# First batch: roots pair by pair, the later value maxima loaded behind the fifth pair and spread through DRAM at once

## The chip, the cores and the metric

The kernel runs on one core of one Trainium2 chip. The metric is the device time of one execution, in microseconds (us): the kernel before takes 1167.9 us, the median of 3 runs (1166.9 to 1169.97). Times of the trace count from the start of the profiled execution's span. The engines are PE (matrix products), ACT (activations and copies), DVE (vector operations), POOL (here short vector operations and the issue of some transfers) and SP (issue of most transfers). Each engine takes its instructions strictly in the order of its own list, so an instruction that waits holds up everything behind it on that engine.

## The reference

Three layers follow each other. The inputs q, k, v are (4, 12, 448, 64): 4 batches, 12 heads, 448 positions.

```python
def rmsnorm(x, g):
    rms = np.sqrt(np.mean(x * x, axis=-1, keepdims=True) + 1e-06)
    return x / rms * g
q_n, k_n = (rmsnorm(q, g_q), rmsnorm(k, g_k))
scores = scale * np.matmul(q_n, k_n.transpose(0, 1, 3, 2))
scores = scores - np.max(scores, axis=-1, keepdims=True)
attn = np.exp(scores)
attn = attn / (np.sum(attn, axis=-1, keepdims=True) + 1e-09)
x = np.matmul(attn, v)            # to (1792, 768)
h = x @ w_in                      # moe: 768 -> 2048 -> 768
x = (h * (1.0 / (1.0 + np.exp(-1.702 * h)))) @ w_out
h = x @ w_in2                     # moe2: 768 -> 2048 -> 768
out = (np.maximum(h, 0.0) + alpha * np.minimum(h, 0.0)) @ w_out2
```

The weights of the layers come as 64-bit words and are turned into single precision on the chip.

## The kernel before

**Stages.** Attention works on pairs of heads, six pairs in a batch, 24 in all. Batch 0 runs in single precision, the other three with numbers split into two half-precision parts. The first 205 us or so hold all of batch 0's attention, and beside it the conversion of the first layer's two weights (`weights`, named w1i and w1o in the trace; each piece of a row is loaded by SP at line 222, turned on ACT at line 147 and on DVE at lines 163 and 164, and reduced at line 244). From there on PE multiplies through the layers, with the attention of batch b + 1 laid between the products of batch b.

**Roots of a pair.** `normalize` takes the sums of squares of a pair's q and k (ACT line 401, DVE line 403) and then takes the reciprocal roots on POOL: one addition (line 404), one starting value (line 407) and three rounds of four short instructions (lines 411 to 414), 14 instructions in all. For batch 0 the roots go to `prep_pair`, which multiplies q and k by them on DVE (line 438, the tile qn), transposes the products on PE (lines 445 and 447) and copies them out on ACT (line 448). Before the change the first and the second pair have roots of their own, and the third and fourth, and the fifth and sixth, share a set of 14 instructions with twice the columns.

**The maxima of v.** Batches 1 to 3 need one scale each: the largest absolute value of v, rounded down to a power of two (mv), and a number made of its reciprocal (av). `v_scale` loads a batch's v in 8 pieces of 168 KB from POOL's queue (line 310, tile vst, two buffers), and ACT reduces each piece to a column (line 311). So a piece's load waits for the piece two before it to be reduced. `v_scales` then reduces the 8 columns on DVE, and `partition_max` spreads the maximum over the 128 partitions by a diagonal matrix on DVE (line 117, tile diag), a product with ones on PE (line 119, tile pm) and a reduction on DVE (line 120). The first use of av for batch 1 is `split` of a pair's v (tile vs), at 190.6 us.

**Order.** The code is written as generators that are stepped in turn, and a scheduler puts the instructions of each engine in an order, from the code's order, priorities and modelled times. The loads of v's pieces are written late in the code, with `issue_after(rooted[1].ins)`: they may be issued once the second pair's roots are done. The scheduler puts them as early as that lets it. On SP, the loads of w1o's 32 half rows stand one behind the other; each waits for one of four buffers.

Of the kernel before, what the change touches and what calls it, by code (L numbers as in the profile page):

```python
# [9 lines left out]
F32 = mybir.dt.float32  # L10
# [4 lines left out]
ALU = mybir.AluOpType  # L15
AX = mybir.AxisListType.X

EXP_MASK = 0x7F800000
VN = 8
# [16 lines left out]
SQB = 2  # L36
# [20 lines left out]
def attention_moe_kernel(  # L57
# [17 lines left out]
    nc = tc.nc  # L75
    B, H, S, D = q.shape
# [4 lines left out]
    NP = H // 2  # L81
# [5 lines left out]
    const = ctx.enter_context(tc.tile_pool(name="const", bufs=1))  # L87
    big = ctx.enter_context(tc.tile_pool(name="big", bufs=1))
    dram = ctx.enter_context(tc.tile_pool(name="dram", bufs=1, space=bass.MemoryType.DRAM))
    small = ctx.enter_context(tc.tile_pool(name="small", bufs=2))  # L90
# [11 lines left out]
    def pow2floor(dst, src):  # L102

        nc.vector.tensor_scalar(out=dst, in0=src, scalar1=1e-30, scalar2=None, op0=ALU.max)  # L104
        nc.vector.tensor_scalar(
            out=dst.bitcast(I32), in0=dst.bitcast(I32), scalar1=EXP_MASK, scalar2=None, op0=ALU.bitwise_and
        )

    def scaled_reciprocal(dst, src, c):

        nc.vector.tensor_scalar(out=dst, in0=src, scalar1=1.0 / c, scalar2=None, op0=ALU.mult)
        nc.vector.reciprocal(out=dst, in_=dst)

    def partition_max(dst, col):

        diag = small.tile([128, 128], BF16, tag="diag", name="diag", bufs=1)
        nc.vector.tensor_scalar(out=diag, in0=ident, scalar1=col, scalar2=None, op0=ALU.mult)
        pm = ps_m.tile([128, 128], F32, tag="m", name="pm")
        nc.tensor.matmul(out=pm, lhsT=ones, rhs=diag, start=True, stop=True)
        nc.vector.tensor_reduce(out=dst, in_=pm, op=ALU.max, axis=AX)  # L120
# [133 lines left out]
    def later_rows(w, d, other):  # L254

        nj = w.shape[1]
        return lambda j: w[:, j + d].rearrange("p e n -> p (e n)").bitcast(F32) if j + d < nj else other(j)
# [9 lines left out]
    att_p = att.enter_context(tc.tile_pool(name="att_p", bufs=2))  # L267
# [5 lines left out]
    g_col = const.tile([128, 1], F32, name="g_col")  # L273
    mv = const.tile([128, B], F32, name="mv")
    av = const.tile([128, B], F32, name="av")

    def gains():
        gq = small.tile([128, D], F32, tag="gq", name="gq", bufs=1)
# [18 lines left out]
    def v_scales(b, col):  # L297
        one = small.tile([128, 1], F32, tag="vone", name="vone")
        nc.vector.tensor_reduce(out=one, in_=col, op=ALU.max, axis=AX)
        pow2floor(one, one)  # L300
        partition_max(mv[:, b:b + 1], one)
        scaled_reciprocal(av[:, b:b + 1], mv[:, b:b + 1], 2.0 ** 13)

    def v_scale(b):
        flat = v[b].rearrange("h s d -> (h s d)").rearrange("(p n) -> p n", p=128)
        n = flat.shape[1] // VN
        col = small.tile([128, VN], F32, tag="vcol", name="vcol")
        for i in range(VN):
            t = raw_p.tile([128, n], F32, tag="vst", name="vst")
            nc.gpsimd.dma_start(out=t, in_=flat[:, i * n:(i + 1) * n])  # L310
            nc.scalar.activation(out=t, in_=t, func=AF.Abs, accum_out=col[:, i:i + 1])
        v_scales(b, col)

    raws = {}
    rawv = {}
# [67 lines left out]
    rooted = {}  # L383
# [295 lines left out]
    def first_pairs():  # L679

        steps = attention([4 * P + r for P in range(NP) for r in range(2)])
        for i, _ in enumerate(steps):
            P, r = divmod(i, 2)
            if P >= NP:
                yield
                continue
            if r == 0:
                prep = prep_pair(P + 1) if P + 1 < NP else iter(())
            next(prep, None)
            if r == 0 and P % 2 == 0 and P + 2 < NP:  # L690
                normalize(P + 2, P + 3)
            if r == 1:
                if P + 1 + QKB < NP:
                    load_qk(P + 1 + QKB)
                if P + 3 < NP:
                    load_v(P + 3)
            yield
# [456 lines left out]
    if True:  # L1154
        make_identity(nc, ident)
        nc.vector.memset(ones, 1.0)
        nc.vector.tensor_copy(out=identf, in_=ident)
        load_qk(0)
        gains()
        load_v(0)  # L1160
        load_qk(1)
        load_v(1)
        g0 = big.tile([128, KF, 2, S], F16, tag="g", name="g0")
        stage = g0.rearrange("p m e t -> p (m e t)").bitcast(F32)
        parts = stage[:, 0:R1I * 1024].bitcast(I32).rearrange("p (i n t) -> p i n t", i=R1I, t=2)
        raw1o = g0.rearrange("p m e t -> p m (e t)").bitcast(I32)[:, KF - 4 * R1O:, FIRST:].rearrange("p m (n t) -> p m n t", t=2)

        def num1i(j):
            if j == KD - 1:
                return stage[:, 5120:5120 + FF]  # L1170
            return held.bitcast(F32)[:, (j - 3) * FF:(j - 2) * FF]

        def num1o(j):
            if j == KF - 2:
                return att_p.tile([128, 2 * NT2 * D], F32, tag="ph", name="num1o", bufs=PHB)[:, 0:DM]
            return raw_p.tile([128, 2 * NT2 * D], F32, tag="qk", name="num1o", bufs=QKB)[:, 0:DM]

        w1i_steps = weights(
            moe_w_in, "w1i", lambda: w1i, later_rows(w1i, 3, num1i), lambda t: parts[:, t % R1I], 4, R1I, 2.0 ** -14, scales,
            G1I  # L1180
        )
        w1o_steps = weights(
            moe_w_out, "w1o", lambda: w1o, later_rows(w1o, 2, num1o), lambda t: raw1o[:, 4 * (t % R1O):4 * (t % R1O) + 4], 2,
            R1O, 2.0 ** -25, scales, G1O
        )
        next(w1i_steps)
        normalize(0)
        for _ in prep_pair(0):
            pass
        for P in range(2, 1 + QKB):  # L1190
            load_qk(P)
        load_v(2)
        normalize(1)
        for _ in first_pairs():
            for _ in range(W_RATE):
                next(w1i_steps, None)
        for _ in w1i_steps:
            pass
        v_scales(0, v0)
        first_x()  # L1200
        moe1_scales(0)
        for P in range(NP, NP + 2):
            load_qk(P)
            load_v(P)
        n1o = 0
        steps = attention([4 * P + r for P in range(NP) for r in range(2, 4)])
        for i, _ in enumerate(steps):
            pairs = max(0, (i - LAG + 1) // 2)
            rows = KF - 2 if pairs >= 4 else (HOLD + pairs * HELD) // (2 * DM) - 2
            while n1o < min(1 + 2 * rows + 3 * (rows // 2), (i + 1) * W1O_RATE, 57):  # L1210
                next(w1o_steps)
                n1o += 1
            if i >= M_AT and i - M_AT < KF:
                first_in(slice(0, FIRST), i - M_AT, g0, None)
            if i == VS_AT:
                for b in range(1, B):
                    with tc.issue_after(rooted[1].ins):
                        v_scale(b)
        while n1o < 57:
            next(w1o_steps)  # L1220
            n1o += 1
        for m in range(len(range(2 * NP + LAG)) - M_AT, KF):
            first_in(slice(0, FIRST), m, g0, None)
        with tc.issue_after(loads["w1o"][W1O_HOLD].ins):
            normalize(NP, NP + 1)
            for _ in prep_pair(NP):
                pass
            load_qk(NP + 2)
            load_qk(NP + 3)
            load_v(NP + 2)  # L1230
        att_steps = other_batches()
        done = 4 * NP
        late = late_weights(ctx, att)
        for b in range(B):
            last = min(NU, 4 * NP * (b + 2)) + LAG
            first = done
            got = None
            for i, _ in enumerate(moe1(b) if b else first_moe1(g0)):
                lead = 0 if b else B1_AT
                want = first + (last - first) * min(1.0, max(0.0, i + 1 - lead) / (PACE[b] * TICKS - lead))  # L1240
                while done < min(want, NU + LAG):
                    next(att_steps)
                    done += 1
                if b == B - 1:
                    for _ in range(1 if i < 2 * KF else 2):
                        if got is None or i >= 2 * KF:
                            got = next(late, None)
        second_layer(late)
# [30 lines left out]
```

## Time and profile before

| what | value |
|---|---|
| median of 3 runs | 1167.9 us (1166.9 to 1169.97) |
| the profiled execution's own time | 1169.73 us |
| its span, first to last instruction | 1168.0 us |
| mean granted clock of PE | 0.961 |
| PE busy, 292 to 1168 us | 857.2 of 876 us |
| PE busy, 0 to 205 us | 145.6 of 205 us |

The first 205 us are unlike the rest. From 292 us on PE is busy 98% of the time, so there the order of the other engines matters little. In the first 205 us PE stands for 59 us, and DVE (168.3 us) and ACT (142.4 us) are busy beside it. The profile attributes a wait to the instruction that came last.

### The profile page before, as it was taken

How to read it: one execution, taken by the hardware profiler on the slowest of the kernel's cores; microseconds unless marked ns; L12 is line 12 of the kernel's file. 1: busy time of each engine (PE TensorE's matmuls, PEld its weight loads, DVE VectorE, ACT ScalarE, POOL GpSimd, SP SyncE). 2: the span in 40 equal slices, each digit the busy share in tenths (PEclk: the TensorE clock that was granted, in tenths of full speed). 3: DMA queues.
4: the chain of work that ended last, by engine and by line, in shares of the span. 5: the costliest groups of instructions: out<-in, count | busy, mean ns of one | idle time of the engine just before them, and what ended most of it. 6: DMA issues, size and time to landing. Idle time of an engine off the chain costs nothing.

```text
span 1168.0 us, 18355 instructions
## 1 busy us (share of the span) xinstructions
PE 1072.6 (92%) x6755; PEld 586.6 (50%) x6755; DVE 810.1 (69%) x1407; ACT 682.0 (58%) x1396; POOL 169.6 (15%) x336
## 2 busy tenths in 40 slices
PE   3587779778998999999999999999999999999998
PEld 1243447743444445545555455444444477666665
DVE  6979987897788976567633957499977222978351
ACT  4789666576888886578733554256545323645220
POOL 3321001575543432210000000000000000000000
PEclk9677889998999999999999999999999999999999
DMA  7975542358898876665555801555533413353011
GB/s 244 273 213 143 148 136 71 89 100 165 173 175 171 148 121 143 139 120 97 102 123 155 302 4 52 201 202 195 183 103 120 138 68 120 100 179 105 29 32 31
DMA packets 235274, 158.05 MB, mean 135 GB/s; under 512 B 167728, under 2 KB 214448, under 8 KB 235184
## 3 DMA queue, kind: packets, MB, share of 16 engines
q1 hardware_dynamic: 228912, 141.21, 46.5%
q0 software_dynamic: 6272, 15.67, 5.2%
q8 instruction: 53, 0.87, 0.3%
q14 instruction: 37, 0.30, 0.1%
HBM read 92.22 MB, written 25.69 MB: 101 GB/s over the span
## 4 chain that ended last, share of the span: by engine, by line
PE 49%; DVE 17%; DMA 13%; ACT 10%; issue 7%; POOL 3%; SPq 1%; ACTq 0%; DVEq 0%; POOLq 0%
PE op L1062 16%; PE h L902 10%; PE yp L796 10%; PE hp L773 5%; ACT pr L529 3%; PE xp L626 2%; DVE ph L598 2%; DVE nm L510 2%; DMA w2raw<-in_moe_w_in_dram 2%; DMA g<-in_moe_w_out_dram 2%; ACT ph L571 2%; DVE g L140 1%; DMA t<-hl 1%; PE hp L727 1%; DMA yr<-y_dram 1%
## 5 line engine op out<-in xcount | busy, mean ns | idle before, releaser
L796 PE MATMUL yp<-g,w1o 128*128 128x448 f16 x1152 | 228.3, 356 | 0.6 <-DVE g L737 0.6
L902 PE MATMUL h<-x,w2i 128*128 128x512 f16 (+1 forms) x1152 | 220.6, 354 | 3.5 <-DVE rm_w2o L104 2.2
L773 PE MATMUL hp<-x,w1i 128*128 128x448 f16 x864 | 169.8, 353 | 1.8 <-DVE t L782 1.8
L902 PEld LDWEIGHTS <-w2i 128*128 128x128 f16 x1152 | 113.1, 98 | 110.0 <-issue 6.3
L796 PEld LDWEIGHTS <-w1o 128*128 128x128 f16 x1152 | 110.2, 98 | 112.5 <-issue 14.1
L773 PEld LDWEIGHTS <-w1i 128*128 128x128 f16 x864 | 81.9, 98 | 83.9 <-issue 9.9
L598 DVE SCALAR_TENSOR_TENSOR ph<-pr,sm,ph 128x448 f16<-128x448 f32 x126 | 89.6, 739 | 27.6 <-ACT ph L571 27.4
L510 DVE TENSOR_REDUCE nm<-sp 128x2 f32<-128x896 f32 x96 | 92.5, 964 | 10.5 <-PE sp L505 8.4
L907 ACT ACTIVATE pos<-h,sign 128x512 f32<-128x512 f32 (+1 forms) x64 | 40.1, 628 | 91.8 <-PE h L902 84.7
L529 ACT ACTIVATE pr<-sp,nm,c_s 128x448 f32<-128x448 f32 x126 | 90.1, 718 | 3.8 <-DVE ph L598 2.2
L571 ACT ACTIVATE ph<-pr,sm 128x448 f16<-128x448 f32 x126 | 77.9, 660 | 18.1 <-DVE sm L568 18.0
L1062 PEld LDWEIGHTS <-even 128*128 128x128 f16 x672 | 65.7, 98 | 43.4
L908 DVE SCALAR_TENSOR_TENSOR pos<-h,slope,pos 128x512 f32<-128x512 f32 (+1 forms) x64 | 43.4, 680 | 61.0 <-ACT pos L907 61.0
L727 PE MATMUL hp<-x,w1i 128*128 128x256 f16 (+1 forms) x576 | 63.2, 270 | 10.1 <-DVE g L737 7.6
L1062 PEld LDWEIGHTS <-odd 128*128 128x128 f16 x504 | 49.3, 98 | 32.6
L626 PE MATMUL xp<-pt,vs 128*64 128x256 f16 (+1 forms) x792 | 48.6, 268 | 17.4 <-DMA pt<-ph 15.1
L1062 PE MATMUL op<-w2lo,even 128*128 128x384 f16 x384 | 63.4, 326 | 0.0
L727 PEld LDWEIGHTS <-w1i 128*128 128x128 f16 x576 | 53.8, 102 | 18.5 <-issue 13.8
L505 PE MATMUL sp<-t 64*128 64x448 f16 (+1 forms) x432 | 54.6, 360 | 0.9 <-ACT pr L529 0.9
L626 PEld LDWEIGHTS <-vs 128*64 128x64 f16 x792 | 38.6, 113 | 33.0 <-DMA pt<-ph 14.6
L512 ACT ACTIVATE nm<-nm,c_s 128x2 f32<-128x2 f32 x72 | 20.9, 290 | 47.5 <-DVE nm L510 47.3
L1062 PE MATMUL op<-w2hi,even 128*128 128x384 f16 x288 | 47.5, 326 | 0.0
(239 smaller groups left out, 1650.0 us busy)
## 6 DMA issues: line engine op xcount, KB each, us to landing
g<-in_moe_w_in_dram SPq DMA_DIRECT2D x24, 512.0 KB, 5.4
g<-in_moe_w_out_dram SPq DMA_DIRECT2D x32, 384.0 KB, 3.7
w2raw<-in_moe_w_in_dram SPq DMA_DIRECT2D x24, 512.0 KB, 5.6
w2raw<-in_moe_w_out_dram SPq DMA_DIRECT2D x16, 768.0 KB, 6.3
g_dram<-pos SPq DMA_DIRECT2D x48, 256.0 KB, 2.0
gp<-g_dram SPq DMA_DIRECT2D x8, 1024.0 KB, 7.1
odd<-g_dram SPq DMA_DIRECT2D x6, 1024.0 KB, 5.4
y_dram<-y SPq DMA_DIRECT2D x24, 224.0 KB, 2.6
```

The lines of the kernel that those rows point to most:

```text
L505: nc.tensor.matmul(out=sp[:, j, 0:S] if n == 2 else sp[ds, 0, 0:S], lhsT=qt[ds] if n == 2 else qt[ds, 64:128], rhs=kt[ds, 0:S], start=(i = ...
L510: nc.vector.tensor_reduce(out=nm[:, 0:n], in_=sp[:, 0:n, 0:S], op=ALU.max, axis=AX, negate=True)
L529: nc.scalar.activation(out=pr[i], in_=sp[:, i, 0:S], func=AF.Exp, bias=nm[:, i:i + 1], scale=c_s if u >= 4 * NP else 1.0, accum_out=sm[:, ...
L571: nc.scalar.activation(out=ph[:, i, 0:S], in_=pr[i], func=AF.Copy, scale=sm[:, i:i + 1])
L598: nc.vector.scalar_tensor_tensor(out=ph[:, i, S:2 * S], in0=pr[i], scalar=sm[:, i:i + 1], in1=ph[:, i, 0:S], op0=ALU.mult, op1=ALU.subtract)
L626: nc.tensor.matmul(out=xp[64 * j:64 * j + 64, t:t + n], lhsT=vs[ks, j, c], rhs=pt[ks, 7 * j + kc, 0:n] if b else pt[ks, kc, o:o + n], star ...
L727: nc.tensor.matmul(out=ps, lhsT=w1i[:, kk, e, m * 128:(m + 1) * 128], rhs=xs[0, kk][:, f, cols], start=(i == 0), stop=(i == 3 * KD - 1))
L773: nc.tensor.matmul(out=ps, lhsT=w1i[:, kk, e, m * 128:(m + 1) * 128], rhs=x[:, f], start=(n == 0), stop=(n == 3 * KD - 1))
L796: nc.tensor.matmul(out=ps, lhsT=w1o[:, m, e, j * 128:(j + 1) * 128], rhs=g[:, m, f], start=(n == 0), stop=(n == 3 * KF - 1))
L902: nc.tensor.matmul(out=ps, lhsT=w2i[:, kk, e, m * 128:(m + 1) * 128], rhs=x2[kk][:, f], start=(c == 0), stop=(c == 3 * KD - 1))
L908: nc.vector.scalar_tensor_tensor(out=pos, in0=ps, scalar=slope[:, m:m + 1], in1=pos, op0=ALU.mult, op1=ALU.max)
L1062: nc.tensor.matmul(out=ps, lhsT=ops[:, o, m, f], rhs=rhs[:, e], start=(c == 0), stop=(c == 3 * KH - 1))
```

## The change

It has three parts. First, in batch 0 each pair gets roots of its own: `normalize(P + 2)` at every pair, instead of `normalize(P + 2, P + 3)` at every second one. Second, the loads of the later batches' v may be issued behind the fifth pair's roots (`rooted[4]`), no more behind the second's. Third, the three maxima are taken together at the end: the columns of the three batches lie in one tile (vcols), one reduction gives 3 numbers in each partition (vmax), these are written to DRAM (v_line, 128 x 3) and read back by every partition (vrow, 384 numbers each), and one reduction over the partitions gives the three mv. `partition_max` is no more called for batches 1 to 3.

```diff
+    vcols = const.tile([128, B - 1, VN], F32, name="vcols")
...
-        col = small.tile([128, VN], F32, tag="vcol", name="vcol")
+        col = vcols[:, b - 1]
         for i in range(VN):
             t = raw_p.tile([128, n], F32, tag="vst", name="vst")
             nc.gpsimd.dma_start(out=t, in_=flat[:, i * n:(i + 1) * n])
             nc.scalar.activation(out=t, in_=t, func=AF.Abs, accum_out=col[:, i:i + 1])
-        v_scales(b, col)
+
+    def later_v_scales():
+        n = B - 1
+        one = small.tile([128, B - 1], F32, tag="vone", name="vmax")
+        nc.vector.tensor_reduce(out=one, in_=vcols, op=ALU.max, axis=AX)
+        pow2floor(one, one)
+        line = dram.tile([128, n], F32, name="v_line")
+        row = att_p.tile([128, 128 * n], F32, tag="sq", name="vrow", bufs=SQB)
+        nc.sync.dma_start(out=line, in_=one)
+        nc.sync.dma_start(out=row, in_=line.rearrange("p b -> (p b)").partition_broadcast(128))
+        nc.vector.tensor_reduce(out=mv[:, 1:B], in_=row.rearrange("q (p b) -> q b p", b=n), op=ALU.max, axis=AX)
+        scaled_reciprocal(av[:, 1:B], mv[:, 1:B], 2.0 ** 13)
...
-            if r == 0 and P % 2 == 0 and P + 2 < NP:
-                normalize(P + 2, P + 3)
+            if r == 0 and P + 2 < NP:
+                normalize(P + 2)
...
                 for b in range(1, B):
-                    with tc.issue_after(rooted[1].ins):
+                    with tc.issue_after(rooted[4].ins):
                         v_scale(b)
+                later_v_scales()
```

The scheduler makes a new order of it on every engine up to about 400 us; behind that the lists are the same but for line numbers. Three places matter below.

POOL, from the end of the second pair's roots on, before (ss, rs and tn are a set's sums, roots and helper):

```order
L414 TENSOR_TENSOR rs<-tn,rs 128x14
L310 DMA vst<-in_v_dram 128x336 x4
L404 TENSOR_SCALAR ss<-ss 128x28
...
L413 TENSOR_SCALAR tn<-tn 128x28
L310 DMA vst<-in_v_dram 128x336
L414 TENSOR_TENSOR rs<-tn,rs 128x28
L310 DMA vst<-in_v_dram 128x336 x3
L404 TENSOR_SCALAR ss<-ss 128x28
```

The same place now, with numbers, since the sets (third to sixth pair: 250, 352, 475, 603) read alike otherwise:

```order
L426 TENSOR_TENSOR rs_211<-tn_212,rs_211 128x14
L416 TENSOR_SCALAR ss_250<-ss_250 128x14
...
L416 TENSOR_SCALAR ss_352<-ss_352 128x14
...
L416 TENSOR_SCALAR ss_475<-ss_475 128x14
...
L426 TENSOR_TENSOR rs_483<-tn_484,rs_483 128x14
L311 DMA vst_1476<-in_v_dram 128x336
...
L311 DMA vst_1485<-in_v_dram 128x336
L416 TENSOR_SCALAR ss_603<-ss_603 128x14
```

Four loads of v stood ahead of the third pair's roots and the rest were strewn between the shared sets; now the roots of the third, fourth and fifth pair stand ahead of every load, four loads ahead of the sixth pair's roots, and the other 20 behind them.

DVE, ahead of the product with the third pair's roots (qn_343), before:

```order
L403 TENSOR_REDUCE ss_249<-sq_256 128x7
L403 TENSOR_REDUCE ss_249<-sq_259 128x7
L510 TENSOR_REDUCE nm_372<-sp_369 128x2
L163 TENSOR_SCALAR w1i_77<-w1i_77 128x512
L164 SCALAR_TENSOR_TENSOR w1i_77<-g0_143,w1i_77 128x512 x2
L179 SCALAR_TENSOR_TENSOR w1i_77<-w1i_77,inv_w1i_145 128x2048
L450 TENSOR_REDUCE v0_96<-w1o_78 128x1
L163 TENSOR_SCALAR w1i_77<-w1i_77 128x512
L403 TENSOR_REDUCE ss_457<-sq_458 128x7
L403 TENSOR_REDUCE ss_457<-sq_461 128x7
L163 TENSOR_SCALAR w1i_77<-w1i_77 128x512
L438 TENSOR_TENSOR qn_343<-qk_189,rs_263 128x2x7x64
```

The same place now (the product is qn_338, ss_352 the fourth pair's sums, ss_475 the fifth's):

```order
L415 TENSOR_REDUCE ss_352<-sq_353 128x7
L163 TENSOR_SCALAR w1i_77<-w1i_77 128x512
L550 RECIPROCAL sums_233<-sums_233 128x4
L171 TENSOR_SCALAR inv_w1i_146<-rm_w1i_145 128x1
L415 TENSOR_REDUCE ss_352<-sq_356 128x7
L522 TENSOR_REDUCE nm_390<-sp_387 128x2
L163 TENSOR_SCALAR w1i_77<-w1i_77 128x512
L164 SCALAR_TENSOR_TENSOR w1i_77<-g0_144,w1i_77 128x512
L462 TENSOR_REDUCE v0_97<-w1o_78 128x1
L450 TENSOR_TENSOR qn_338<-qk_190,rs_258 128x2x7x64
L415 TENSOR_REDUCE ss_475<-sq_476 128x7
L164 SCALAR_TENSOR_TENSOR w1i_77<-g0_144,w1i_77 128x512
```

The long instruction of line 179 and the fifth pair's sums stood ahead of the third pair's product and stand behind it now.

SP, from the end of the first weight's loads on, now (before, the 32 loads of the second weight stood together, but for two small copies ahead of the last):

```order
L222 DMA g<-in_moe_w_in_dram 128x1024 x2
L222 DMA g<-in_moe_w_out_dram 128x4x192 x11
L321 DMA v_line<-vmax 128x3
L222 DMA g<-in_moe_w_out_dram 128x4x192 x8
L322 DMA vrow<-v_line 128x384
L222 DMA g<-in_moe_w_out_dram 128x4x192 x11
```

The write of the maxima stands behind 11 of the 32 half rows, their reading back 8 half rows later; on DVE the last instruction of vmax stands behind the conversion of 7 half rows and the reduction of vrow behind that of 18.

## Rows read from the trace of the kernel before

**Rows 1.** Page, part 1: busy time, share of the span and instructions of each engine.

```profile
PE 1072.6 (92%) x6755; PEld 586.6 (50%) x6755; DVE 810.1 (69%) x1407; ACT 682.0 (58%) x1396; POOL 169.6 (15%) x336
```

**Rows 2.** Busy time by stretch: stretch, length, busy per engine, clock, DMA share, GB/s.

```profile
20.00:60.00 40.00, 22.70 (x100) 11.53 (x96) 37.91 (x70) 28.24 (x68) 13.66 (x31) 0.68 0.93 282
60.00:130.00 70.00, 52.51 (x283) 26.27 (x284) 59.55 (x130) 57.76 (x139) 10.71 (x24) 0.79 0.63 170
130.00:205.00 75.00, 65.19 (x496) 44.74 (x497) 61.90 (x151) 49.49 (x110) 3.86 (x6) 0.88 0.40 113
205.00:218.00 13.00, 10.03 (x107) 9.71 (x105) 10.62 (x27) 5.08 (x10) 7.01 (x18) 0.91 0.14 37
```

**Rows 3.** Timeline of POOL, roots: start, busy time, instruction, [idle before <- releaser].

```profile
9.38 0.26 POOL L404 TENSOR_SCALAR ss<-ss 128x14 f32<-128x14 f32 x1 [8.08 <-DVE ss L403]
...
13.29 0.22 POOL L414 TENSOR_TENSOR rs<-tn,rs 128x14 f32<-128x14 f32 x1
...
33.15 0.28 POOL L404 TENSOR_SCALAR ss<-ss 128x28 f32<-128x28 f32 x1 [3.99 <-DVE ss L403]
...
34.13 1.57 POOL L412 TENSOR_TENSOR tn<-tn,ss 128x28 f32<-128x28 f32 x1
35.78 2.15 POOL L413 TENSOR_SCALAR tn<-tn 128x28 f32<-128x28 f32 x1
...
41.51 0.26 POOL L414 TENSOR_TENSOR rs<-tn,rs 128x28 f32<-128x28 f32 x1
```

**Rows 4.** Timeline of DVE around the third pair's product.

```profile
28.63 1.13 DVE L403 TENSOR_REDUCE ss<-sq 128x7 f32<-128x448 f32 x2
...
34.31 1.28 DVE L164 SCALAR_TENSOR_TENSOR w1i<-g,w1i 128x512 int32<-128x512 int32 x2
35.52 2.34 DVE L179 SCALAR_TENSOR_TENSOR w1i<-w1i,inv_w1i 128x2048 f16<-128x2048 f32 x1
...
41.80 1.09 DVE L438 TENSOR_TENSOR qn<-qk,rs 128x896 f32<-128x896 f32 x1 [1.63 <-POOL rs L414]
```

**Rows 5.** Groups of DVE instructions, 20 to 218 us: count | busy, mean ns.

```profile
L120 DVE TENSOR_REDUCE mv<-pm 128x1 f32<-128x128 f32 x4 | 1.1, 282 | 0.4 <-PE pm L119 0.4
L117 DVE TENSOR_SCALAR diag<-ident,vone 128x128 bf16<-128x128 bf16 x4 | 1.0, 243 | 0.0
L112 DVE RECIPROCAL av<-av 128x1 f32<-128x1 f32 x4 | 0.6, 153 | 0.0
L104 DVE TENSOR_SCALAR vone<-vone 128x1 f32<-128x1 f32 x4 | 0.6, 142 | 0.0
```

**Rows 6.** Waits of DVE, 20 to 205 us: total us, times, longest.

```profile
DVE g L737 <- ACT t L736: 4.5, 4, 2.1
...
DVE qn L438 <- POOL rs L414: 2.6, 2, 1.6
...
DVE vone L299 <- ACT vst L311: 0.8, 1, 0.8
```

**Rows 7.** Timeline of PE and then DVE, 169 to 180 us.

```profile
169.01 0.27 PE L119 MATMUL pm<-diag,ones 128*128 128x128 bf16 x1 [3.08 <-DVE diag L117]
171.54 0.26 PE L119 MATMUL pm<-diag,ones 128*128 128x128 bf16 x1 [2.27 <-DVE diag L117]
...
179.65 0.42 DVE L737 SCALAR_TENSOR_TENSOR g<-t,hp 128x256 f32<-128x256 f32 x1 [2.15 <-ACT t L736]
```

**Rows 8.** Loads of v's pieces: POOL's issues, ACT's wait in 20 to 205 us.

```profile
66.69 0.59 POOL L310 DMA_DIRECT2D vst<-in_v_dram  x1 [2.86 <-ACT vst L311]
...
105.83 0.54 POOL L310 DMA_DIRECT2D vst<-in_v_dram  x1 [4.02 <-ACT vst L311]
...
ACT vst L311 <- DMA vst<-in_v_dram: 6.3, 6, 3.9
```

**Rows 9.** Landing of lines 127 (write) and 128 (spread); SP's w1o loads.

```profile
DMA to landing us min/median/max: 7.3/7.9/9.3
...
DMA to landing us min/median/max: 4.1/4.4/4.9
...
92.10 94.81 SPq L222 DMA_DIRECT2D g<-in_moe_w_out_dram  x31
```

## The prediction

> **What bounds the kernel now.** I read the table of engines first: PE is busy 92% of the span [rows 1], so the whole leaves little room. The table by stretch says where the room is. From 20 to 205 us PE works only 22.7 of 40, 52.5 of 70 and 65.2 of 75 us, while DVE works 37.9, 59.6 and 61.9 us of them [rows 2]. So the change acts in a part that DVE paces: its idle time from 20 to 218 us is 2.1 + 10.4 + 13.1 + 2.4 = 28.0 us, and every instruction that the change leaves in place must still pass through it. What can be won there is DVE work that goes and DVE idle time that goes. By 218 us, when w1o's scales are formed, the orders before and after hold the same DVE instructions but for those of the maxima; work moved back within the stretch is paid within it. Behind it the work is the same and each part needs the one ahead, so I let a shift at 218 us reach the end in full.
>
> Then the timelines at the places that the change touches. POOL's roots of the third pair start at 33.15 us, when the fourth pair's sums are there too, and end at 41.77 [rows 3], though the third pair's sums are done at 28.63 + 1.13 = 29.76 [rows 4]. DVE's product waits for them until 41.80; but DVE itself stood for only 1.63 us of that, since its list held w1i's work ahead of the product [rows 4]. That is the main reading: PE and ACT lose much here, the pacing engine little.
>
> **The change part by part.**
>
> *Roots pair by pair.* A set of 14 columns took 9.38 to 13.51, 4.1 us, for the first pair [rows 3]. The third pair's can start at 29.8 and end near 33.9 instead of 41.8. They are not used then: on DVE ten instructions stand between the third pair's last sums and the product, two of them (lines 510 and 403) with waits on other engines, and I put the product at 36, six us earlier. The 1.63 us of standing go, and line 179 (2.34 us) and the fifth pair's sums move behind the product. I count -1.6 us. POOL gets two more sets, 2 x 4.1 us, at a time when it stands anyway; they cost nothing, since POOL is busy 13.7 of 40 us in that stretch [rows 2]. If that cover fails, it is by the length of a set: the shared set took 8.6 us, with line 412 at 1.57 and line 413 at 2.15 us, exactly while DVE ran lines 164 and 179 (34.31 to 35.59, 35.52 to 37.86) [rows 3, 4]. Now only two runs of line 164 (0.64 each) stand on DVE in that time, so a set is 4.1 to 5.4 us, done by 35.2, still ahead of 36. Bounds of this term: -2.6 (all waits on roots from 20 to 205 us [rows 6]) to +2.4 (roots as long as before, 29.8 + 8.6 = 38.4, against 36).
>
> [...]
>
> *Maxima, DVE's work.* For three batches seven instructions each go: lines 299 and 112 at 0.153, 104, 105 and 111 at 0.142, 117 at 0.243, 120 at 0.282 us (299 taken like 112, and 105 and 111 like 104) [rows 5]: 3 x 1.257 = 3.8 us. In come one each of the five short ones on three columns, 0.73, and the reduction of vrow with three times the columns of line 120, between 0.28 and 0.85, taken as 0.55 since it must read with a stride: 1.3 us. Neighbours overlap by 0.07 us (35.52 starts ahead of 35.59 [rows 4]), so 21 x 0.07 = 1.5 and 6 x 0.07 = 0.4 come off. Net 2.3 - 0.9: -1.4 us; bounds -2.5 and -1.0. Line 299's wait of 0.8 us on a piece of v [rows 6] goes too: -0.8.
>
> *Maxima, PE's wait.* PE stood 3.08 and 2.27 us at two of the products with ones [rows 7], with the attention of the last pairs behind them in its list. DVE felt it as 2.15 us at 179.65, where a product's activation came late. That wait goes: -2.1; bounds 0 (something else is late there, w1o's half rows) and -4.5 (all waits of line 737 on ACT [rows 6]).
>
> *Maxima through DRAM.* A write of one column landed after 7.3 to 9.3 us, a spread read after 4.1 to 4.9 [rows 9]; together 11.4 to 14.2. SP can't be held by the read, since 8 half rows stand between, and they pass at 94.8 / 31 = 3.06 us each [rows 9]: 24 us. On DVE 11 half rows lie between vmax and vrow's reduction, 33 us. So the chain is covered: 0. If the cover were gone it would cost at most 14.2. The first use, the split of v, is at 190 us, far behind. The write could hold SP while vmax is late; that is the next term.
>
> *Loads of v behind the fifth pair's roots.* Sums of three pairs one after another put the fifth pair's roots near 45 us, so the first two pieces land near 50, where ACT's list has them, just ahead of the fourth pair's copies from PE; then the sixth pair's roots, and 20 loads from about 56 us. Before, 14 loads took 66.69 to 105.83, 13 steps of 3.0 us [rows 8]; 20 at that pace end at 116, landed near 120, and the split of batch 0's x, behind the 23rd piece on ACT, wants them near 118. ACT waited 6.3 us for pieces before, in 6 waits [rows 8]. The stretch 20 to 60 us, where the DMA engines are busy 0.93 [rows 2], loses eight pieces, and 60 to 130, at 0.63, gains them. Bounds: -2 (less load early) to +8 (each of the 20 late by 0.4 us in a list without slack, and DVE held at vmax). I take +1.5, near the lower end, because the old waits were of the same size with the same pace.
>
> Sum: -1.6 - 1.4 - 0.8 - 2.1 + 1.5 = -4.4 us. The profiled execution took 1169.73 us, which gives 1165.3; it lies 1.8 us above the median of the runs shown, so against the median 1167.9 - 4.4 = 1163.5 us.
>
> **The rivals.**
>
> *The room is taken by something else.* The third pair's product comes six us earlier, but DVE's work does not shrink, and w1o's conversion, which now lies later, is what ends last at 205 us. For it: DVE is busy 83 to 95% from 20 to 205 us, and the standing at the roots was 1.6 us. Against it: 28 us of idle time are there. Only the work that went counts: 1167.9 - 1.4 = 1166.5, no change.
>
> *ACT stands on v's pieces.* All 24 pieces now have to pass ACT between about 50 and 118 us, two of them right ahead of the fourth pair's copies. With 3.0 us a piece and no slack ACT falls behind by the upper bound of 8 us; batch 0's x, and with it the first products of w1i, come that much later, and vmax holds DVE and then SP. It decides once pieces are later than about 0.3 us each. Then -5.9 + 8 plus DVE's hold at vmax, some 2 us: 1172, slower.
>
> *PE's wait counts in full.* If the chain through PE and ACT, not DVE, ends last between 160 and 205 us, the 5.35 us at the two products go whole, and the six us at the third pair's product count more than the 1.6 us that DVE saw. Then about -10: 1158.
>
> **How the numbers follow.** Forecast 0.45 (1160.5 to 1166), the room taken 0.24, ACT standing 0.18, PE's wait in full 0.13. A measurement of this kernel can tell about 0.3% (3.5 us) from no change: 1164.4 to 1171.4. Faster: 0.39 of the forecast's 0.45 and the 0.13, 0.52. Same: 0.06 of the forecast, the 0.24 and a little of ACT standing, 0.31. Slower 0.17. The range leaves out the far end of each side: 1155 to 1172.
>
> **What would show it.** Right: POOL's third set starts near 30 us and no load of v before 45; the product qn of the third pair near 36; no PE wait at line 119 from 160 to 172 us; DVE's wait at the reduction of vrow is nothing; w1o's scales (line 198) come 4 to 5 us earlier than the 218 us of now, and the rest of the trace is shifted by as much. Wrong: ACT waits on pieces of v well over 6 us in total, or DVE at vmax; a head start at 125 us that is gone at 218; or a shift at 218 that the later layers don't keep.

## The result and the profile after

The changed kernel takes 1155.54 us (median of 6 runs, 1153.11 to 1158.49), the kernel before 1168.93 us (6 runs) beside it: a ratio of 0.9888 (95% interval 0.9865 to 0.9912), 13.4 us faster. A later measurement of the same two gave 0.9825 (0.9794 to 0.9856). The two intervals don't meet, so a repeat can differ by 0.6%, more than an interval says; the gain is 1.1 to 1.8%. The forecast was 1163.5 us with a range of 1155 to 1172. The direction held. The range held by half a microsecond, which is luck: the later measurement's 1153.0 us lies outside it. The size, 4.4 us, was a third of what came.

The profiled execution took 1154.34 us, with a span of 1152.6. First its table of engines, to be set beside [rows 1]:

```profile
PE 1063.4 (92%) x6752; PEld 581.2 (50%) x6752; DVE 802.6 (70%) x1392; ACT 681.2 (59%) x1396; POOL 180.9 (16%) x364
```

PE does the same work but for three small products, yet it is busy 9.2 us less: in places its products ran faster, as the next section shows. DVE is busy 7.5 us less, POOL 11.3 us more (its two further sets of roots). Then the stretches of [rows 2], in the kernel after (length, busy time of PE, PE's weight loads, DVE, ACT, POOL, granted clock of PE as a share of full speed, DMA share, GB/s):

```profile
20.00:60.00 40.00, 26.15 (x110) 13.13 (x108) 36.48 (x66) 27.98 (x62) 21.44 (x61) 0.64 0.92 273
60.00:130.00 70.00, 48.62 (x294) 26.04 (x292) 59.82 (x122) 57.40 (x144) 11.09 (x21) 0.82 0.64 170
130.00:205.00 75.00, 66.25 (x573) 48.59 (x572) 68.79 (x167) 53.69 (x118) 10.92 (x22) 0.98 0.45 124
205.00:218.00 13.00, 11.14 (x128) 9.70 (x126) 10.82 (x23) 9.71 (x21) 8.68 (x13) 1.00 0.68 178
```

The change shows in the third row. From 130 to 205 us DVE's idle time fell from 13.1 to 6.2 us, PE got 573 products done in place of 496, and its granted clock rose from 0.88 to 0.98. In the two rows ahead of it DVE's busy time differs by 1.4 and 0.3 us only, though the next table shows a head start from there too.

The same is seen in when certain instructions start (us; "first split" is the scale first_sc with which batch 0's x is split; the 7th and 8th columns are DVE's products with the activation of w1i's first products, line 737 before and 749 after; w1o's scales are line 198; the last two are PE's first products with w1o for batches 0 and 1):

| kernel | first split | 7th column | 8th column | w1o's scales | batch 0, w1o | batch 1, w1o |
|---|---|---|---|---|---|---|
| before | 124.0 | 166.6 | 179.7 | 218.2 | 243.1 | 430.3 |
| after | 114.2 | 160.8 | 165.2 | 207.6 | 229.3 | 417.2 |
| difference | -9.8 | -5.8 | -14.4 | -10.6 | -13.8 | -13.1 |

Four of the 9.8 us at the first split are gone by the 7th column; from the 7th to the 8th column 8.6 us come in at one stroke. That is where the products with ones stood on PE. By w1o's scales 3.8 of the 14.4 us are lost again.

### The profile page after: what moved, and what is told of

It is laid out like the page before. It is cut to its first block, busy times and chain, and to the rows that moved or that the text cites. A ratio compares the mean times of both kernels' runs of the same rounds, so it can differ in the third digit from the quotient of the medians.

```text
span 1152.6 us, 18352 instructions
## 1 busy us (share of the span) xinstructions
PE 1063.4 (92%) x6752; PEld 581.2 (50%) x6752; DVE 802.6 (70%) x1392; ACT 681.2 (59%) x1396; POOL 180.9 (16%) x364
## 4 chain that ended last, share of the span: by engine, by line
PE 53%; DVE 16%; DMA 13%; issue 7%; ACT 6%; POOL 4%; SPq 1%; ACTq 0%; POOLq 0%; DVEq 0%
PE op L1074 16%; PE yp L808 13%; PE hp L785 10%; PE h L914 7%; DMA pt<-ph 3%; PE xp L638 3%; PE sp L517 2%; DMA g<-in_moe_w_out_dram 2%; DMA t<-hl 2%; DMA yr<-y_dram 1%; DMA vst<-in_v_dram 1%; DVE pos L920 1%; DMA qk<-in_q_dram 1%; ACT pr L541 1%; DVE g L140 1%
## 5 line engine op out<-in xcount | busy, mean ns | idle before, releaser
L610 DVE SCALAR_TENSOR_TENSOR ph<-pr,sm,ph 128x448 f16<-128x448 f32 x126 | 86.6, 715 | 25.6 <-ACT ph L583 25.6
L638 PE MATMUL xp<-pt,vs 128*64 128x256 f16 (+1 forms) x792 | 49.8, 271 | 15.3 <-DMA pt<-ph 14.9
L739 PEld LDWEIGHTS <-w1i 128*128 128x128 f16 x576 | 51.8, 99 | 20.7 <-issue 17.1
L524 ACT ACTIVATE nm<-nm,c_s 128x2 f32<-128x2 f32 x72 | 20.9, 290 | 48.5 <-DVE nm L522 48.4
L598 PE MATMUL tp<-identf,pr 128*128 128x128 f32 x168 | 31.5, 325 | 17.8 <-ACT ptf L603 7.3
```

The costliest lines, as they stand in the source:

```text
L610: nc.vector.scalar_tensor_tensor(out=ph[:, i, S:2 * S], in0=pr[i], scalar=sm[:, i:i + 1], in1=ph[:, i, 0:S], op0=ALU.mult, op1=ALU.subtract)
L638: nc.tensor.matmul(out=xp[64 * j:64 * j + 64, t:t + n], lhsT=vs[ks, j, c], rhs=pt[ks, 7 * j + kc, 0:n] if b else pt[ks, kc, o:o + n], star ...
L739: nc.tensor.matmul(out=ps, lhsT=w1i[:, kk, e, m * 128:(m + 1) * 128], rhs=xs[0, kk][:, f, cols], start=(i == 0), stop=(i == 3 * KD - 1))
```

## What happened between the 7th and the 8th column

[Rows 7] show PE standing 3.08 and 2.27 us at two of the products with ones. Here are rows of the kernel before that follow them, from PE's timeline (transposes tp, short products rp, values xp, the products hp of w1i's 8th column):

```profile
171.60 1.06 PE L586 MATMUL tp<-identf,pr 128*128 128x128 f32 x4
...
173.35 0.69 PE L552 MATMUL rp<-identf,sums 128*64 128x128 f32 x4 [0.69 <-ACT ptf L591]
173.98 0.48 PE L548 MATMUL rp<-identf,sums 64*64 64x64 f32 x4
174.39 1.55 PE L626 MATMUL xp<-ptf,w1o 128*64 128x192 f32 x8
175.87 3.23 PE L727 MATMUL hp<-x,w1i 128*128 128x256 f16 x18
```

And the same work in the kernel after:

```profile
160.53 0.44 PE L564 MATMUL rp<-identf,sums 128*64 128x128 f32 x4
160.90 0.33 PE L560 MATMUL rp<-identf,sums 64*64 64x64 f32 x4
161.16 0.87 PE L638 MATMUL xp<-ptf,w1o 128*64 128x192 f32 x8
161.97 2.14 PE L739 MATMUL hp<-x,w1i 128*128 128x256 f16 x18
...
167.84 0.60 PE L598 MATMUL tp<-identf,pr 128*128 128x128 f32 x4
170.35 0.44 PE L564 MATMUL rp<-identf,sums 128*64 128x128 f32 x4 [1.92 <-ACT ptf L603]
```

Each takes 1.5 to 1.8 times as long before. The stretches of 5 us show a lower granted clock beside that; the kernel before, 165 to 180 us:

```profile
165.00:170.00 5.00, 1.19 (x6) 0.35 (x6) 4.09 (x15) 2.90 (x6) 0.00 (x0) 0.79 0.19 40
170.00:175.00 5.00, 2.76 (x17) 1.83 (x18) 5.00 (x16) 2.83 (x8) 0.00 (x0) 0.50 0.65 197
175.00:180.00 5.00, 5.00 (x34) 3.46 (x32) 2.85 (x11) 0.96 (x3) 0.00 (x0) 0.69 0.29 79
```

and the kernel after at the same work and, in the last line, behind its 8th column:

```profile
155.00:160.00 5.00, 4.70 (x32) 2.42 (x30) 4.93 (x12) 3.39 (x10) 0.00 (x0) 1.00 0.52 154
160.00:165.00 5.00, 4.83 (x46) 3.76 (x48) 4.98 (x19) 2.88 (x8) 0.00 (x0) 1.00 0.38 87
...
170.00:175.00 5.00, 4.65 (x31) 3.08 (x32) 5.00 (x12) 3.44 (x8) 0.00 (x0) 0.66 0.39 105
```

While PE stood at the products, busy 1.19 of 5 us, its granted clock fell to 0.50, and it stayed there behind them; taken by single microseconds it reads 1.00 from 164 to 167, 0.95 in the next, 0.50 from 168 to 178 and 0.93 from 178 to 179 us. So the three products cost: standing 3.08 + 2.27, themselves 0.23 + 0.27 + 0.26, and behind them, by rows of equal work, 0.46 (tp) + 0.40 (rp) + 0.68 (xp) + 1.09 (hp) = 2.6 us of longer rows at the clock of 0.50: 8.7 us together. The gap from the 7th to the 8th column shrank from 179.65 - 166.57 = 13.08 to 4.44 us, by 8.6. The forecast had 2.1 us for this. The changed kernel pays a smaller price of the same kind behind its 8th column, where PE stands 1.92 us for ACT and the clock of the stretch is 0.66; that may be part of the 3.8 us that it loses there.

## The experiments

All numbers are ratios to the kernel before, run beside each on the same chip (its medians there were 1170.9 to 1172.2 us), with 95% intervals. The changed kernel itself gave 0.9888 and 0.9825 at two times, so rows of different chips are compared to about 0.6% only. The theories named in the expectations: A, the forecast's sum, by what DVE does and waits; B, PE's standing at the products with ones, and what is queued behind it, is the price; C, the early product of the third pair counts nearly whole; D, roots and loads gain together, ahead of 125 us.

| kernel | ratio | interval | chip |
|---|---|---|---|
| roots alone | 1.0068 | 1.0041 to 1.0096 | 8 |
| loads alone | 1.0085 | 1.0052 to 1.0118 | 8 |
| maxima alone | 0.9825 | 0.9793 to 0.9858 | 8 |
| maxima alone, again | 0.9807 | 0.9775 to 0.9839 | 7 |
| roots and loads | 1.0033 | 1.0007 to 1.0060 | 9 |
| loads and maxima | 0.9934 | 0.9904 to 0.9963 | 9 |
| roots and maxima | 0.9983 | 0.9962 to 1.0005 | 9 |
| all three, again | 0.9825 | 0.9794 to 0.9856 | 7 |
| all, maxima by three products | 0.9965 | 0.9934 to 0.9996 | 8 |
| all, maxima by one product | 0.9931 | 0.9902 to 0.9960 | 9 |
| all, and three unused products | 1.0038 | 1.0009 to 1.0067 | 7 |
| maxima alone, loads behind the shared roots of pairs 3, 4 | 0.9915 | 0.9889 to 0.9941 | 7 |

**One part alone.** To the kernel before, roots only:

```diff
-            if r == 0 and P % 2 == 0 and P + 2 < NP:
-                normalize(P + 2, P + 3)
+            if r == 0 and P + 2 < NP:
+                normalize(P + 2)
```

> The kernel before with the first part alone: roots pair by pair; v's loads still behind the second pair's roots, each maximum by a product with ones. Theory A (DVE paces, each part is worth the DVE work and the DVE idle time that it takes away): -1.6 us against before. Theory C (the product of the third pair, 5.7 us earlier in the changed kernel, counts nearly whole, and most of the 9.8 us by which the split of batch 0's x starts earlier comes from it): -6 to -9 us. Theory D (parts one and two only work together, since loads that stand between the sets of roots hold up POOL and ACT): within 2 us of before.

Measured: 1.0068, 8 us slower. A, C and D all miss, though the third pair's product came at 34.7 us in place of 41.8: seven us early there, and the first split at 124.2 where it was before. Loads only:

```diff
-                    with tc.issue_after(rooted[1].ins):
+                    with tc.issue_after(rooted[4].ins):
```

> The kernel before with the second part alone: v's loads behind the root set that holds the fifth pair, which with shared roots is the set of the fifth and sixth pair, so that all 24 loads stand behind all roots of batch 0. Theory A: +1.5 us (ACT gets all 24 pieces late). Theory C: the same, 0 to +3. Theory D: -3 to -6 us, since the loads no longer stand in the way of the third pair's roots and of the first weight's loads; the product of the third pair should then be some us ahead of 41.80 even with shared roots.

Measured: 1.0085, 10 us slower, more than A said; the first split came at 129.5 (the profile is of its fastest run, 1174.8 us). The maxima only:

```diff
+    vcols = const.tile([128, B - 1, VN], F32, name="vcols")
...
-        col = small.tile([128, VN], F32, tag="vcol", name="vcol")
+        col = vcols[:, b - 1]
...
-        v_scales(b, col)
...
+                later_v_scales()
```

> The kernel before with the third part alone: the three maxima together, through DRAM, roots shared and loads behind the second pair's roots. Theory A: -1.4 - 0.8 - 2.1 = -4.3 us. Theory B (PE's standing at the products with ones, 5.35 us, counts in full, and what ends last from 160 to 205 us is PE and ACT): -7 to -10 us. Theories C and D (the gain is made ahead of 125 us): -1 to -3 us.

Measured: 0.9825, 20 us faster: all of the gain. B named the right part and was still too low; A's -4.3 is refuted as a size, C and D are refuted. The profile gives B its place: no product with ones is left on PE between the 7th and the 8th column, and they lie 170.76 - 167.06 = 3.7 us apart. But at w1o's scales this kernel is only 4.5 us ahead of the kernel before (213.65 against 218.20); the rest of the 20 us comes behind them, and B's working has nothing there. The repeats below come back to it.

**One part taken out.** From the changed kernel, first without the maxima's new way:

```diff
-        col = vcols[:, b - 1]
+        col = small.tile([128, VN], F32, tag="vcol", name="vcol")
...
+        v_scales(b, col)
...
-                later_v_scales()
```

> The changed kernel without its third part: roots pair by pair and v's loads behind the fifth pair's roots, each maximum by its own product with ones. Alone the three parts gave +0.7%, +0.85% and -1.75%. If the parts add and the way of the maxima is worth 20 us wherever it stands: 1.0063 of before, some 7 us slower. If PE's standing at the products is worth what the kernel with the three products together lost (0.8%), and roots and loads together do no harm: 0.997 to 1.000, no change. Theory A (the sum of the forecast): -1.6 + 1.5 = 0.

Measured: 1.0033. Roots and loads together cost 4 us, 1 to 7 us by the interval: between the first two expectations, with A's 0 just outside. The products are back, and the gap from the 7th to the 8th column is 174.66 - 162.02 = 12.6 us again, though the first split came at 117.0. Then with shared roots, and with the early loads:

```diff
-            if r == 0 and P + 2 < NP:
-                normalize(P + 2)
+            if r == 0 and P % 2 == 0 and P + 2 < NP:
+                normalize(P + 2, P + 3)
```

> The changed kernel without its first part: shared roots, all of v's loads behind them, maxima through DRAM. If the parts add: 0.0085 - 0.0175, so 0.991 of before (-10.5 us), slower than the maxima alone by 10 us. If the loads behind all roots cost only because the maxima then come late and PE stands at their products: as fast as the maxima alone, 0.982. Theory A: -4.3 + 1.5 = -2.8 us.

Measured: 0.9934, near what addition gives.

```diff
-                    with tc.issue_after(rooted[4].ins):
+                    with tc.issue_after(rooted[1].ins):
```

> The changed kernel without its second part: roots pair by pair, v's loads behind the second pair's roots, maxima through DRAM. If the parts add: 0.0068 - 0.0175, so 0.989 of before (-12.5 us). If roots pair by pair cost only through the maxima: 0.982. Theory A: -1.6 - 4.3 = -5.9 us.

Measured: 0.9983, slower than any of the three expectations. The parts don't add: roots or loads singly cost 0.7 to 1.6% beside either way of the maxima (1.1 and 1.6% beside the new way, where chips 8 and 9 are compared), both together 0.3% or less where one chip ran the kernels compared. The waits of ACT from 20 to 130 us show what the single ones share. Loads alone, then loads and maxima:

```profile
ACT w1i L147 <- DMA g<-in_moe_w_in_dram: 8.3, 4, 4.5
ACT w1o L147 <- DMA g<-in_moe_w_in_dram: 6.4, 4, 2.9
```

```profile
ACT w1i L147 <- DMA g<-in_moe_w_in_dram: 8.9, 5, 3.6
ACT w1o L147 <- DMA g<-in_moe_w_in_dram: 6.6, 4, 3.2
```

These are pieces of the first weight that come late: 14.7 and 15.5 us in all; with roots alone 7.6, with roots and maxima 9.4, against 3.9 before and 3.7 after. In these four the first split comes at 124 to 131 us, in the kernels with both or neither at 114 to 124. So the two parts are no gain each; they avoid each other's harm. The late pieces go with that harm, but are not shown to be all of it: with roots alone the first split comes where it came before (124.2 against 124.0), and yet 8 us are lost. Why the pieces are late in just these orders was not tested.

**The way of the maxima, with roots and loads as changed.** First the three maxima together, but by three products:

```diff
-        line = dram.tile([128, n], F32, name="v_line")
-        row = att_p.tile([128, 128 * n], F32, tag="sq", name="vrow", bufs=SQB)
-        nc.sync.dma_start(out=line, in_=one)
-        nc.sync.dma_start(out=row, in_=line.rearrange("p b -> (p b)").partition_broadcast(128))
-        nc.vector.tensor_reduce(out=mv[:, 1:B], in_=row.rearrange("q (p b) -> q b p", b=n), op=ALU.max, axis=AX)
+        for b in range(n):
+            partition_max(mv[:, b + 1:b + 2], one[:, b:b + 1])
```

> The changed kernel, but the three maxima, still taken together at the end, are spread by three products with ones on PE (as before) in place of the way through DRAM. Theory B: PE stands again for the diagonals, DVE for the products, so most of the gain is lost: within 4 us of the kernel before. Theory A: DVE gets 3 x (0.24 + 0.28) us more and 0.55 less, and PE's wait (2.1) may return: +1 to +3 us against the changed kernel. Theories C and D: 0 to +1.5 us against the changed kernel, 10 to 13 us faster than before.

Measured: 0.9965, 4 us faster than before, about as B had it. PE's waits from 115 to 230 us in it:

```profile
PE pm L119 <- DVE diag L117: 5.1, 2, 3.0
```

Its first split starts with that of the changed kernel (114.17 and 114.24), its 7th column is 1.4 us earlier (159.34 and 160.76), its 8th is at 171.17 in place of 165.20, and w1o's scales are at 213.36 in place of 207.56: the 6 us lost at one place are still there 40 us on. So DVE does not take up what PE loses. (By the ratios it is 9 to 16 us slower than the changed kernel; what goes beyond these 6 us comes behind w1o's scales.) Then one product of 384 columns, with the three diagonals made in a row; the same five lines go, and these come in:

```diff
+        diag = att_p.tile([128, n, 128], BF16, tag="sq", name="vdiag", bufs=SQB)
+        for b in range(n):
+            nc.vector.tensor_scalar(out=diag[:, b], in0=ident, scalar1=one[:, b:b + 1], scalar2=None, op0=ALU.mult)
+        pm = ps_m.tile([128, n, 128], F32, tag="m", name="pm")
+        nc.tensor.matmul(out=pm, lhsT=ones, rhs=diag, start=True, stop=True)
+        nc.vector.tensor_reduce(out=mv[:, 1:B], in_=pm, op=ALU.max, axis=AX)
```

> The changed kernel with the three maxima spread by one product of 384 columns on PE, in place of the way through DRAM: DVE makes three diagonals and then one reduction, and PE stands at most once for them. Theory B (the time goes by PE's standing, where one product waited behind the other for its diagonal, 2.97 + 2.13 us in the kernel with three products, and by what is queued behind it): within 3 us of the changed kernel, 0.988 to 0.991 of before. Theory A (the DVE work and DVE's waits for the product count): 0.5 to 1 us slower than the changed kernel by the three diagonals, the same 0.988 to 0.990. A product of any kind disturbs, by its place in PE's list: 0.995 to 0.998, as with three.

Measured: 0.9931, between the expectations. PE does not stand at this product:

```profile
156.88 0.34 PE L323 MATMUL pm<-vdiag,ones 128*128 128x384 bf16 x1
```

and the 8th column comes at 164.96, as in the changed kernel. B holds up to there. But w1o's scales are at 214.8: later PE stood 5.4 us behind a column whose sum was late on DVE (released by line 750). What brought that about is left open. Last, the changed kernel with the maxima through DRAM and used from there, and the three products beside it, unread:

```diff
+    unused = const.tile([128, B - 1], F32, name="unused")
...
+        for b in range(n):
+            partition_max(unused[:, b:b + 1], one[:, b:b + 1])
```

> The changed kernel, the maxima through DRAM and used from there, and beside it the three products with ones on PE once more, into a tile that nothing reads. Theory B (PE's standing for the diagonals, and what is queued behind the products on PE, is the price): as slow as the kernel with three products, 0.995 to 0.998 of before, and w1o's scales at 212 to 214 us in place of 207.6. Theory A (DVE's work alone): three diagonals, three reductions, 1.6 us: 0.990 to 0.991, scales at 209. If it were the late arrival of the maxima where they are used: as the changed kernel, 0.988 to 0.990.

Measured: 1.0038, beside 0.9825 of the changed kernel on the same chip. That is the plainest result here: the maxima come the same way as in the changed kernel, and three products that nobody needs, with their diagonals and reductions on DVE (1.6 us by theory A), take the whole gain. PE's timeline in this kernel:

```profile
167.22 0.22 PE L119 MATMUL pm<-diag,ones 128*128 128x128 bf16 x1 [2.74 <-DVE diag L117]
169.70 0.27 PE L119 MATMUL pm<-diag,ones 128*128 128x128 bf16 x1 [2.27 <-DVE diag L117]
...
172.42 1.55 PE L641 MATMUL xp<-ptf,w1o 128*64 128x192 f32 x8
173.90 4.01 PE L742 MATMUL hp<-x,w1i 128*128 128x256 f16 x18
```

and its stretches:

```profile
165.00:170.00 5.00, 0.51 (x4) 0.39 (x4) 5.00 (x18) 2.01 (x3) 0.00 (x0) 0.75 0.70 223
170.00:175.00 5.00, 4.44 (x26) 2.57 (x25) 4.84 (x13) 3.58 (x10) 0.00 (x0) 0.50 0.32 80
```

Standing, the clock at 0.50, 18 products in 4.01 us in place of 2.14: the picture of the kernel before. The 7th and 8th columns are 179.71 - 167.24 = 12.5 us apart. It lost more than B said, 25 us by the ratios and 22 by the medians. 8 of these lie here. Another 4.5 are there at the first split already (119.4 against 114.9 in the changed kernel beside it), with DVE's list the same up to there; w1o's scales come 14.6 us later (222.5 against 207.9), and the others come behind them. What does not lie here is not explained by PE's standing as such.

**The changed kernel and the maxima alone, on one chip.**

> The changed kernel once more, beside the three that follow: 0.987 to 0.991 of before. Its part up to w1o's scales (line 198, 207.6 us) is compared with that of the kernel with both ways of the maxima.

> The third part alone once more, on the same chip as the changed kernel: if it is the better version, 0.980 to 0.986 of before and 5 us or more below the changed kernel; if the first run was favoured by the chip, the two are within 3 us. In the stretch from w1o's scales to the second batch's last products PE should again stand for pieces that come by transposing DMAs some 6 us in place of 15.

Measured: 1153.0 us and 1150.9 us, 0.9825 and 0.9807, within 3 us. The changed kernel did better than was expected of its repeat. The third part alone is as good as all three, not shown better. The repeat also says how firm the stretch behind w1o's scales is. From these scales to batch 1's first products with w1o the changed kernel took 209.7 us in its first profile and 201.1 in the second, with the same instructions. PE's waits there for pieces that come by transposing DMAs, in the first and then in the second:

```profile
PE xp L638 <- DMA pt<-ph: 14.9, 9, 3.3
```

```profile
PE xp L638 <- DMA pt<-ph: 8.0, 7, 2.3
```

So 7 of these 8.6 us are one wait that changes from run to run, and a difference of that size behind 208 us can't be put down to a change from one profile. All the profiles together say more. In this stretch the six kernels that have the three products with ones took 209.8 to 217.4 us, with 12.6 to 16.4 us of that wait; the seven profiles without them took 195.3 to 211.6 us, with 5.9 to 14.9. (From the 7th to the 8th column it is 8.6 to 13.1 us against 3.6 to 6.6.) The ranges overlap by 2 us only, so with the products the stretch behind w1o's scales tends to be longer too. The maxima alone took 195.3 and 197.2 us there in its two profiles, the kernel before 212.1. That is 17 of the 22 us by which the first of these profiles is shorter: PE has 6.8 us less left to do (busy 182.3 in place of 189.1 us) and stands 9.2 us less at that wait (5.9 in place of 15.1). Whether and how the products on PE bring this about was not tested.

**A try at a better one.** The maxima alone, loads behind the shared roots of the third and fourth pair:

```diff
-                    with tc.issue_after(rooted[1].ins):
+                    with tc.issue_after(rooted[2].ins):
```

> A try at a better version: the third part alone, with v's loads behind the shared roots of the third and fourth pair, no more ahead of them. If what stands ahead of these roots on POOL costs: 3 to 6 us better than the third part alone, 0.978 to 0.981 of before. If a later issue costs by ACT's late pieces, as with all loads behind all roots (0.993): between the two, 0.985 to 0.990.

Measured: 0.9915, a little above the second expectation; ACT waits 13.4 us for pieces of the first weight, as in the kernels above, and the first split is at 132.9. No version was found that beats the changed kernel beyond the intervals. One standing of the same kind is left in it, at the product with ones for the first weight, where the kernel before stood 0.69 us; no run took it away:

```profile
108.39 0.29 PE L119 MATMUL pm<-diag,ones 128*128 128x128 bf16 x1 [6.35 <-DVE diag L117]
```

## Why the prediction was right in sign and short in size

*Roots pair by pair, -1.6.* The steps came as forecast. POOL, start and duration of the rows that answer to [rows 3] and of the first loads of v:

```profile
29.48 0.26 POOL L416 TENSOR_SCALAR ss<-ss 128x14 f32<-128x14 f32 x1 [9.40 <-DVE ss L415]
...
34.30 0.22 POOL L426 TENSOR_TENSOR rs<-tn,rs 128x14 f32<-128x14 f32 x1
34.49 0.53 POOL L416 TENSOR_SCALAR ss<-ss 128x14 f32<-128x14 f32 x1
...
38.45 2.19 POOL L424 TENSOR_TENSOR tn<-tn,ss 128x14 f32<-128x14 f32 x1
...
48.51 1.34 POOL L311 DMA_DIRECT2D vst<-in_v_dram  x2
...
61.21 0.60 POOL L311 DMA_DIRECT2D vst<-in_v_dram  x1 [1.13 <-ACT vst L312]
```

DVE beside it:

```profile
36.08 1.09 DVE L450 TENSOR_TENSOR qn<-qk,rs 128x896 f32<-128x896 f32 x1
...
38.22 2.34 DVE L179 SCALAR_TENSOR_TENSOR w1i<-w1i,inv_w1i 128x2048 f16<-128x2048 f32 x1
```

The set starts at 29.5 (forecast 29.8), ends at 34.5 (by 35.2), and the product starts at 36.08 (36), with no wait. (Sixteen of DVE's instructions, not ten, stood between the third pair's sums and the product; the time was right all the same.) One row of POOL was long again beside a long one of DVE: line 424 took 2.19 us, from 38.45 to 40.64, while DVE ran line 179, from 38.22 to 40.56; the median of its 18 rows of this form is 0.22. That set, the fourth pair's, took 8.2 us. It fell on a set that had time, its product starting at 45.08, and the third pair's set took 5.0 us, so the +2.4 of the far bound did not come. Why POOL's row is long there was not tested. Together with the loads' +1.5 this term was near nothing, and the measured pairs agree: +0.3% (1 to 7 us) without the new maxima, nothing within 3 us with them. Taken by itself, each term was wrong: alone the parts cost 8 and 10 us, with pieces of the first weight late, and the forecast had no such cost. It hardly changed the number here only because both parts were made, and that is luck.

*Maxima, DVE's work, -1.4.* Right in direction, at the far bound in size: up to w1o's scales DVE runs the same instructions but for those of the maxima, and is busy 176.6 us in place of 179.2, so -2.5. The reduction of vrow was 0.70 us, not 0.55, and it had a wait that the forecast put at nothing:

```profile
154.26 0.70 DVE L323 TENSOR_REDUCE mv<-vrow 128x3 f32<-128x384 f32 x1 [0.94 <-DMA vrow<-v_line]
```

*Maxima, PE's wait, -2.1 (0 to -4.5).* This is the term that was mis-sized: it is -8.6. Two steps failed. The first took DVE's wait, 2.15 us, as the measure of what PE lost, since "DVE paces". But DVE's list holds the sums of the columns, the columns come from PE in order, and DVE was busy at the other work of the list meanwhile: its wait shows only the rest that it could not fill. In the kernel with three products joined, 6 us lost on PE were 6 us at w1o's scales. The second step left out what comes behind the standing: 2.6 us of longer rows at the clock of 0.50. With 8.6 in place of 2.1 the forecast's sum is -10.9; w1o's scales came 10.6 us early. That these agree so well is partly chance: 5.8 us were there at the 7th column already, more than the terms ahead of it give, and 3.8 were lost behind the 8th.

*Maxima through DRAM, 0.* Right: SP issued the write at 129.60 and the reading at 150.27, as far apart as the 8 half rows between them (20.7 us; the estimate was 24), and 0.94 us of wait was all that came through. The kernel with both ways, 1.0038, shows that the way by itself brings no gain: what counts is that the products are off PE.

*Loads behind the fifth pair's roots, +1.5.* The first load went at 48.5, the 20 from 61.2 to 114.6 us. ACT stood longer at pieces of v than [rows 8] show, from 20 to 205 us:

```profile
ACT vst L312 <- DMA vst<-in_v_dram: 12.0, 7, 4.2
ACT t L748 <- PE hp L739: 5.8, 8, 1.2
```

12.0 us is the "well over 6 us" that was named as a sign of the slow rival. It was not one: ACT stood 5.8 us for PE's columns where it had stood 11.6 before, DVE did not wait at vmax (125.03), and the first split came 9.8 us early. So these waits were no price here. The row of before:

```profile
ACT t L736 <- PE hp L727: 11.6, 6, 4.0
```

*The shift is kept.* It was not only kept, it grew: from 10.6 us at w1o's scales to 15.4 at the end of the span, and in the repeat's profile from 10.3 to 22.3. The forecast had nothing behind 218 us but the shift itself. Part of the growth is the wait for transposing DMAs, which changes from run to run; how much of the rest comes of the products being off PE is open.

*The rivals.* "PE's wait counts in full" (1158, chance 0.13) came nearest: 1155.5. It had the right place for the products and left out the clock. The other half of its 10 us, the third pair's product six us early, did not come true: with roots alone that product was seven us early, and the kernel 8 us slower. The rival's case was weighed too low because the table by stretch, in which DVE is busiest, was read as saying who ends last at every point of the stretch.

## What to carry to other kernels

An engine's wait was not priced here by the wait that it caused on the busiest engine (8.6 us against 2.15): follow the next result that everybody needs (here one column of the first product) from kernel to kernel, and take the distance between two of them. A small product on PE that waited for another engine cost its standing here, held up all that was queued behind it, and was followed by the lower clock (0.50, against 1.00 for the same work in the kernel after); three products of 0.25 us cost 8.7 us between two columns. And two edits that cost 8 and 10 us alone cost 4 us or less together, so parts of one change are to be measured in pairs as well as singly.

## What was not expected of the hardware

PE's granted clock stood at 0.50 for a whole stretch of 5 us, from 170 to 175, in which PE's second standing ended, and the 18 products of a column then took 3.23 us (4.01 in the kernel with the unused products) in place of 2.14. The same instructions behind 208 us took 209.7 us in one execution and 201.1 in another, 7 us of it in PE's waits for transposing DMAs (14.9 and 8.0 us).
